# Attention before a gated MLP: products and probability buffers with and without 64 to 192 padding columns

## The chip, the cores and the metric

The kernel runs on one core of a Trainium2 chip. The metric is device time in microseconds (us) for one execution. The engines of a core are named as in the profile: PE is TensorE's matrix multiplication and PEld its loading of the stationary operand (the weights of one product), DVE is VectorE, ACT is ScalarE, POOL is GpSimd, and SP issues the transfers. A product, below, is one matmul instruction: up to 128 x 128 weights, and a moving operand of so many columns.

## The reference

What is computed is block-causal attention over 8 batches of 8 heads, and then a gated MLP on its output:

```python
scores = scale * np.matmul(q, k.transpose(0, 1, 3, 2))      # (8, 8, 576, 576), head_dim 64
mask = block_i >= block_j                                   # blocks of 64 positions
scores = np.where(mask, scores, -1000000000.0)
scores = scores - np.max(scores, axis=-1, keepdims=True)
attn = np.exp(scores)
attn = attn / (np.sum(attn, axis=-1, keepdims=True) + 1e-09)
out = np.matmul(attn, v)                                    # (8, 8, 576, 64)
...
x = out.transpose(0, 2, 1, 3).reshape(4608, 512)
a = x @ w1                                                  # (4608, 1024)
b = x @ w2
h = a * b @ w3
return h @ w_out                                            # (4608, 512)
```

## The kernel before

The heads are taken in 32 pairs, four pairs to a batch. Every float32 value that goes through a product is split in two rounded parts (type fp32r in the profile), a high one and a low one, and products are done as high by high, high by low and low by high. For a head, the tiles `hi` and `lo` hold q and k in this form.

**Scores.** `s_tile` (L226) computes scores transposed, keys on partitions and queries on columns, in five tiles (`S_TILES`, L258): chunk 0 of 128 keys takes two tiles of 288 queries, chunk 1 takes queries 128 to 575, chunk 2 takes 256 to 575, and the fifth tile takes chunk 3 and chunk 4 (64 keys) together. Each part is two products on line L235, one of `hi` and one of `lo`. ACT then takes the exponential twice: to `p` or `rsum` in float32 (L250), and to `ph`, rounded (L251). DVE subtracts the two into `pl`, the low part (L253), and POOL adds `p` to the sums over the keys, `rsum` (L256). Only columns that some query may see are written: chunk 3's exponentials take 192 columns, chunk 4's take 64.

**Probabilities.** `ph` and `pl` have `PW` columns; chunk c begins at `PC[c]`. Between the chunks lie columns of zeros, which POOL writes once (L121), when the tiles of the second stage are opened.

**Values.** `pv` (L281, product on L291) multiplies the values `vs` with `ph` and `pl`, by the list `PV`: chunk 0 in two parts, then chunks 1 to 4. In this version a part of chunk 0, chunk 3 and chunk 4 reach into the zeros, so that each of these products is 256 columns wide. The result gathers in PSUM, in `xps`.

**Order.** The first four pairs (one batch) run while the weights of the MLP come in and are decoded (DVE, L139 to L144); their work is set in order by a scheduler that estimates what each instruction costs, and their values are multiplied in plain float32 (`pv_early`, L275). From pair 4 on, which is the second stage (from some 165 us), PE's order is written out by hand: `PLAN` has one string for the first and one for the second head of a pair; S is a scores tile, V a part of `pv`, F a piece of the MLP (lines L388 and L404), M the maxima of the next pair (`mx`, L182, in bf16), T the sums over the keys (`tot`, L309), and so on. The engines run their instructions in program order, so a product that waits holds all that stands behind it on PE. The MLP lags the attention by a batch, and its last batch stands alone at the end (from some 983 us).

Sums end the pair: DVE transposes `rsum` (`tr`, L304), reduces it (`part`, L305), and PE adds the groups (`tot`, two products of 36 columns). Pair by pair PE's MLP pieces alternate between the first products (`ab`, L388) and the last ones (`o`, L404).

Of the kernel before, what the change touches and what calls it, by code (L numbers as in the profile page):

```python
# [7 lines left out]
F32 = mybir.dt.float32  # L8
# [6 lines left out]
PSUM = bass.MemoryType.PSUM  # L15

P = 128
B, H, S, D = 8, 8, 576, 64
BLK = 64
NB = S // BLK  # L20
NPAIR = H // 2
# [4 lines left out]
NF = DF // P  # L26
HALF = S // 2
RAW = 2 * S + 640
EARLY = NPAIR  # pairs whose work is spread over more engines while the weights come in
SCALE = 0.125  # L30
BIG = 8.0e9

# Columns of a head's probabilities (keys on partitions): a chunk of 128 keys
# takes the queries that may see it; zeros keep every product 256 columns wide.
PC = [128, 704, 1152, 1536, 1920]
PW = 1984
QLO = [0, 128, 256, 384, 512]
# The same without zeros, less the first query.
PE = [0, 448, 768, 960, 1024]


# Order of a head's steps, for the first and the second head of a pair.
PLAN = (
    "B F B F S F S B F F S S F F F S M M V F V V V F R F F V Q N",
    "M A S S A F F S F M M S F F F S M A M V V V F V F F V N Q F R T M F F",
)
# The same for the pairs before the first product of the MLP, while the weights come in.
EARLY_PLAN = (
    "M S S S C S C C C C M S V V B C M M V A V M V M Q B M A B M N",
    "S C C S A S S C S C V V V V V Q N T",  # L50
)
# Steps of the first pair with the MLP beside it that leave the MLP's place empty.
DELAY = 3
# Whether ScalarE makes the roundings of (q and k, q, k, k for the maxima, q for the maxima, v).
CAST = (0, 0, 1, 1, 1, 1)


# [1 line left out]
def block_causal_attention__then__gated_mlp_kernel(ctx, tc, qkv, consts, ident_in, w1, w2, w3t, wout, out_t):  # L59
    nc = tc.nc  # L60
# [4 lines left out]
    work = ctx.enter_context(tc.tile_pool(name="work", bufs=1))  # L65
# [9 lines left out]
    w1l = cpool.tile([P, NC, DF], F32R, name="w1l")  # L75
    wh = cpool.tile([P, NF, DM], F32R, name="wh")
    wl = cpool.tile([P, NF, DM], F32R, name="wl")
    # Per head of a pair: (q, k) with high parts on the head's own half of the
    # partitions and q high, k low on the other; and (q low, k high) on the own
    # half with the rows that shift and mask the scores on the other.  # L80
    hi = [cpool.tile([P, 2, S], F32R, name=f"hi{j}") for j in range(2)]
    lo = [cpool.tile([P, 2, S], F32R, name=f"lo{j}") for j in range(2)]
    w2h = cpool.tile([P, NC, DF], F32R, name="w2h")
    w2l = cpool.tile([P, NC, DF], F32R, name="w2l")
    # Queries of both heads of a pair, block by block on a diagonal.
    qd = cpool.tile([P, NB, P], BF16, name="qd")
    own = [slice(0, D), slice(D, P)]
    oth = [slice(D, P), slice(0, D)]
# [12 lines left out]
    for j in range(2):  # L101
        nc.vector.tensor_copy(lo[j][oth[j]], cst[0:D, 0 : 2 * S].rearrange("p (t s) -> p t s", t=2))
    nc.gpsimd.memset(qd, 0.0)
    # Tiles of the time while the weights come in, and those that take their bytes.
    tl = {}

    def open_early(pool):
# [3 lines left out]
    def open_late():  # L111
        pool = ctx.enter_context(tc.tile_pool(name="late", bufs=1, reuse_waits="tile"))
        tl["late"] = pool
        tl["ph"] = pool.tile([P, PW], F32R, name="ph")
        tl["sum"] = pool.tile([P, S], F32, name="rsum")
        tl["pl"] = pool.tile([P, PW], F32R, name="pl")
        # Values: high part on the columns of the head's own half, low part on the other.
        tl["vs"] = [pool.tile([P, 5, P], F32R, name=f"vs{j}") for j in range(2)]
        for t in (tl["ph"], tl["pl"]):
            for a, b in ((0, PC[0]), (PC[2] + 320, PC[3]), (PC[3] + 192, PC[4])):  # L120
                nc.gpsimd.memset(t[:, a:b].bitcast(F32), 0.0)  # L121
        tl["gh"] = pool.tile([P, NF, HALF], F32R, name="gh")
        tl["gl"] = pool.tile([P, NF, HALF], F32R, name="gl")

    def load_w(dst, src, k):
        """512 columns of float64 words (low, high), as float32.

        Magnitudes below float32's smallest normal become zero.
        """
        t = tl["early"].tile([P, 1024], F32, tag="wraw", name="wraw", bufs=5)  # L130
        u = tl["early"].tile([P, 512], F32, tag="wbits", name="wbits", bufs=6)
        wide = t.bitcast(I32)
        nc.sync.dma_start(out=wide.rearrange("p (k w) -> p k w", k=k), in_=src)
        wide = wide.rearrange("p (c two) -> p c two", two=2)
        low, high = wide[:, :, 0], wide[:, :, 1]
        bits = u.bitcast(I32)
        V = nc.vector
        nc.scalar.activation(u, high.bitcast(F32), AF.Abs)
        V.tensor_scalar(out=u, in0=u, scalar1=2.0**-15, scalar2=None, op0=ALU.max)  # L139
        V.tensor_scalar(out=bits, in0=bits, scalar1=3, scalar2=0x3FFFFFF8, op0=ALU.logical_shift_left, op1=ALU.bitwise_and)  # L140
        V.scalar_tensor_tensor(out=bits, in0=high, scalar=-0x40000000, in1=bits, op0=ALU.bitwise_and, op1=ALU.bitwise_or)  # L141
        if dst is None:
            dst = u.unsqueeze(1)
        V.scalar_tensor_tensor(out=dst.bitcast(I32), in0=low.rearrange("p (k w) -> p k w", k=k), scalar=29,  # L144
                               in1=bits.rearrange("p (k w) -> p k w", k=k), op0=ALU.logical_shift_right, op1=ALU.bitwise_or)
        return u
# [80 lines left out]
    def s_tile(n, j, parts, p_early):  # L227
# [10 lines left out]
        for c, ks, at, q0, q1 in todo:  # L238
# [21 lines left out]
        [(0, 288, 576, 288)],  # L260
        [(1, 128, 576, 128)],
        [(2, 256, 576, 256)],
        [(3, 320, 576, 384), (4, 512, 576, 512)],
    ]
    # (chunk, first column of the probabilities, width, first column in PSUM)
    PV = [(0, 0, 256, 256), (0, PC[0] + 128, 448, 512), (1, PC[1], 448, 512), (2, PC[2], 320, 640),
          (3, PC[3] - 64, 256, 704), (4, PC[4] - 192, 256, 704)]

    def pv_early(n, j, xps, pr):
        for c in range(5):  # L270
# [28 lines left out]
    x_of = {}  # L299

    def sums(n, j, part):
        """Sums over the keys: 32 by 32 transposes, then over the groups of 32 partitions."""
        tr = work.tile([P, S], F32, tag="tr", name=f"tr{n}_{j}")
        nc.vector.transpose(tr, tl["sum"])  # L304
        nc.vector.reduce_sum(part[:, j, :], tr.rearrange("p (b c) -> p b c", c=32), axis=AX.X)  # L305
# [120 lines left out]
    weights = gen_w(wp)  # L426

    def pair(n):
        """The attention of a pair of heads, with what the plan places between its steps."""
        early = n < EARLY  # L430
        x32 = work.tile([P, S], F32, tag="x32", name=f"x32_{n}")
        rr = work.tile([P, S // 32], F32, tag="rr", name=f"rr{n}")
        part = None if early else work.tile([P, 2, S // 32], F32, tag="part", name=f"part{n}")
        last = n + 1 == NN
        masks = iter(()) if last else shift_mask(n + 1)
        own_qk = prep_qk(n, 1)
        next_qk = iter(()) if last else prep_qk(n + 1, 0)
        for j in range(2):
            xps = ps_x.tile([P, 1024], F32, tag="psx", name=f"x{n}_{j}")
            p_early = wp.tile([P, 1600], F32, tag="pe", name=f"pe{n}_{j}") if early else None  # L440
            tiles = iter(S_TILES)
            pvs = (pv_early if early else pv)(n, j, xps, p_early)
            delay = DELAY if n == NPAIR and j == 0 else 0
            for step in (EARLY_PLAN if early else PLAN)[j].split():
                if step == "C":
                    fill(weights, 1)
                    continue
                with tc.high_priority(offset=0) if early else nullcontext():
                    if step == "S":
                        s_tile(n, j, next(tiles), p_early)  # L450
                    elif step == "F":
                        if delay:
                            delay -= 1
                        else:
                            fill(mlp, 1)
                    elif step == "M":
                        fill(masks, 1)
                    elif step == "A":
                        fill(next_qk, 1)
                    elif step == "B":  # L460
                        fill(own_qk, 1)
                    elif step == "V":
                        fill(pvs, 1)
                    elif step == "R":
                        sums(n, j, part)
                    elif step == "N" and early:
                        take_early(n, j, xps, x32, rr)
                    elif step == "N":
                        take(n, j, xps, x32)
                    elif step == "T":  # L470
                        if not early:
                            total(n, part, rr)
                        norm(n, x32, rr)
                        finish_x(n, x32)
                    elif step == "Q" and not last:
                        if n + 1 != NPAIR:
                            prep_v(n + 1, j)
                        if j == 1 and n + 2 < NN:
                            load(n + 2)
# [5 lines left out]
    open_late()  # L485
    for j in range(2):
        prep_v(NPAIR, j)
    # Products of the gated MLP stand between those of the attention, which wait for other engines.
    ctx.enter_context(tc.manual_schedule(engines={mybir.EngineType.PE}))
    mlp = (None for b in range(B - 1) for _ in gen_moe(b))  # L490
    for n in range(NPAIR, NN):
# [52 lines left out]
```

## Time and profile before

| what | value |
|---|---|
| time, median of 3 runs | 1069.15 us (1067.49 to 1069.55) |
| span of the profiled execution, first to last instruction | 1066.6 us |
| the median above that span | 2.55 us |
| PE busy | 986.9 us, 93% |
| DVE busy | 810.3 us, 76% |
| ACT busy | 594.9 us, 56% |
| POOL busy | 601.4 us, 56% |

The profiled execution is shown by its span alone; its time as a run isn't listed, and the 2.55 us are what lies around the span in the median run. Busy times of PE count overlapping matmuls once, and the ends of matmuls are modelled, so starts of successive products tell more than durations do. A wait in brackets behind a row is the engine's idle time ahead of it and what ended it. Times in rows are from the start of the span.

### The profile page before, as it was taken

How to read it: one execution, taken by the hardware profiler on the slowest of the kernel's cores; microseconds unless marked ns; L12 is line 12 of the kernel's file. 1: busy time of each engine (PE TensorE's matmuls, PEld its weight loads, DVE VectorE, ACT ScalarE, POOL GpSimd, SP SyncE). 2: the span in 40 equal slices, each digit the busy share in tenths (PEclk: the TensorE clock that was granted, in tenths of full speed). 3: DMA queues.
4: the chain of work that ended last, by engine and by line, in shares of the span. 5: the costliest groups of instructions: out<-in, count | busy, mean ns of one | idle time of the engine just before them, and what ended most of it. 6: DMA issues, size and time to landing. Idle time of an engine off the chain costs nothing.

```text
span 1066.6 us, 18267 instructions
## 1 busy us (share of the span) xinstructions
PE 986.9 (93%) x6624; PEld 892.7 (84%) x6624; DVE 810.3 (76%) x1432; ACT 594.9 (56%) x1505; POOL 601.4 (56%) x631
## 2 busy tenths in 40 slices
PE   3789778999999999999999999999999999999998
PEld 1444347999998989999999989899999999899998
DVE  7999997878787887778787888877787878886100
ACT  4646566656665656556565656565565656554221
POOL 3324367656575666666565756666665657564211
PEclk9889889999999999999999999999999999999999
DMA  6665421111111001111111110111111111000000
GB/s 214 202 194 191 140 73 36 35 58 36 58 35 54 18 34 47 41 52 36 58 36 58 36 47 19 39 47 42 52 36 58 35 59 36 22 3 18 7 24 23
DMA packets 27196, 61.52 MB, mean 58 GB/s; under 512 B 3361, under 2 KB 19873, under 8 KB 27105
## 3 DMA queue, kind: packets, MB, share of 16 engines
q1 hardware_dynamic: 27104, 60.35, 17.0%
q8 instruction: 52, 0.85, 0.3%
q14 instruction: 40, 0.32, 0.1%
HBM read 50.76 MB, written 9.44 MB: 56 GB/s over the span
## 4 chain that ended last, share of the span: by engine, by line
PE 47%; DVE 34%; ACT 11%; issue 6%; DMA 1%; POOL 1%; ACTq 0%; DVEq 0%; SPq 0%; POOLq 0%
PE ab L388 21%; PE o L404 12%; DVE pl L253 6%; PE s L235 6%; DVE m L186 4%; DVE hi L160 3%; DVE part L305 3%; DVE tr L304 3%; ACT ph L251 3%; DVE g L395 2%; PE x L291 2%; ACT p L250 2%; PE mx L182 2%; PE w L365 2%; DVE wbits L141 2%
## 5 line engine op out<-in xcount | busy, mean ns | idle before, releaser
L256 POOL TENSOR_TENSOR rsum<-rsum,p 128x448 f32<-128x448 f32 x224 | 176.7, 789 | 124.1 <-ACT p L250 116.6
L253 DVE TENSOR_TENSOR pl<-p,ph 128x448 fp32r<-128x448 f32 x168 | 149.1, 901 | 62.2 <-ACT ph L251 61.3
L397 POOL TENSOR_TENSOR gl<-g,gh 128x288 fp32r<-128x288 f32 x128 | 107.5, 840 | 138.0 <-ACT gh L396 135.6
L396 ACT CAST gh<-g 128x288 fp32r<-128x288 f32 x128 | 55.5, 433 | 228.2 <-DVE g L395 228.2
L235 PE MATMUL s<-hi 128*128 128x288 f32 (+4 forms) x384 | 127.8, 344 | 29.0 <-ACT ph L251 21.4
L388 PE MATMUL ab<-xh,w2h 128*128 128x288 f32 x512 | 153.3, 300 | 0.1
L404 PE MATMUL o<-gh,wh 128*128 128x288 f32 x512 | 152.1, 297 | 0.0
L388 PE MATMUL ab<-xh,w1h 128*128 128x288 f32 x512 | 150.9, 295 | 1.1 <-ACT xh L339 1.1
L388 PE MATMUL ab<-xl,w1h 128*128 128x288 f32 x512 | 151.0, 295 | 0.5 <-POOL xl L340 0.5
L388 PE MATMUL ab<-xh,w2l 128*128 128x288 f32 x512 | 150.9, 295 | 0.0
L388 PE MATMUL ab<-xh,w1l 128*128 128x288 f32 x512 | 150.9, 295 | 0.0
L388 PE MATMUL ab<-xl,w2h 128*128 128x288 f32 x512 | 150.9, 295 | 0.0
L404 PE MATMUL o<-gh,wl 128*128 128x288 f32 x512 | 150.8, 295 | 0.0
L404 PE MATMUL o<-gl,wh 128*128 128x288 f32 x512 | 150.7, 294 | 0.0
L186 DVE TENSOR_REDUCE m<-mx 128x1 f32<-128x512 f32 (+6 forms) x320 | 128.1, 446 | 5.0 <-PE mx L182 3.2
L251 ACT ACTIVATE ph<-s 128x288 fp32r<-128x288 f32 x336 | 131.3, 393 | 0.0
L209 POOL TENSOR_TENSOR hi<-raw,hi 64x576 fp32r<-64x576 f32 x64 | 93.7, 1464 | 43.2 <-ACT hi L160 17.8
L291 PE MATMUL x<-ph,vs 128*128 128x256 f32 x336 | 111.6, 340 | 0.1
L250 ACT ACTIVATE p<-s 128x448 f32<-128x448 f32 x224 | 85.4, 381 | 44.6 <-PE s L235 44.3
L235 PE MATMUL s<-lo 128*128 128x288 f32 (+4 forms) x384 | 107.0, 307 | 2.2 <-DMA lo<-ms 1.2
L235 PEld LDWEIGHTS s<-hi 128*128 128x128 f32 (+1 forms) x384 | 70.9, 185 | 45.5 <-ACT ph L251 28.0
L395 DVE TENSOR_TENSOR g<-ab,a 128x288 f32<-128x288 f32 x128 | 57.4, 448 | 66.4 <-PE ab L388 65.5
(77 smaller groups left out, 2558.7 us busy)
## 6 DMA issues: line engine op xcount, KB each, us to landing
raw<-in_qkv SPq DMA_DIRECT2D x32, 896.0 KB
out_t<-o SPq DMA_DIRECT2D x64, 144.0 KB
wraw<-in_w3t SPq DMA_DIRECT2D x16, 512.0 KB
wraw<-in_w SPq DMA_DIRECT2D x16, 512.0 KB
wraw<-in_wout SPq DMA_DIRECT2D x8, 512.0 KB
lo<-ms SPq DMA_DIRECT2D x64, 2.2 KB
cst<-in_consts SPq DMA_DIRECT2D x1, 288.0 KB
ident<-in_ident SPq DMA_DIRECT2D x1, 128.0 KB
```

Source lines behind the costliest of these rows:

```text
L186: nc.vector.reduce_max(m[:, col : col + 1], sc, axis=AX.X)
L209: nc.gpsimd.tensor_tensor(out=hi[j][x, 1, :], in0=rqk[o, 1, :], in1=hi[j][o, 1, :], op=ALU.subtract)
L235: nc.tensor.matmul(t[ks, at : at + q1 - q0], src[:, 1, kr], src[:, 0, q0:q1], start=(s == 0), stop=(s == 1))
L250: nc.scalar.activation(p32, t[ks, at : at + w], AF.Exp, scale=SCALE)
L251: nc.scalar.activation(ph[ks, o : o + w], t[ks, at : at + w], AF.Exp, scale=SCALE)
L253: nc.vector.tensor_tensor(out=low, in0=p32, in1=ph[ks, o : o + w], op=ALU.subtract)
L256: nc.gpsimd.tensor_tensor(out=r, in0=r, in1=p32, op=ALU.add)
L291: nc.tensor.matmul(xps[:, to : to + w], v[:, c, :], pr[:, a : a + w], start=(u < 2 and s == 0), stop=(u in (0, len(PV) - 1) and s == len(p ...
L388: nc.tensor.matmul(t[:, 0:HALF], l[:, c, fs], r, start=(c == 0 and s == 0), stop=(c == NC - 1 and s == 2))
L395: nc.vector.tensor_tensor(out=g32, in0=acc[1][:, 0:HALF], in1=a32, op=ALU.mult)
L397: nc.gpsimd.tensor_tensor(out=gl[:, f, :], in0=g32, in1=gh[:, f, :], op=ALU.subtract)
L404: nc.tensor.matmul(t[:, 0:HALF], l[:, f, es], r[:, f, :], start=(f == 0 and s == 0), stop=(f == NF - 1 and s == 2))
```

## The change

The columns of zeros go. `PC` becomes the running sum of the chunks' own widths and `PW` falls from 1984 to 1600. The six memsets are taken out. In `S_TILES` the fifth tile's part of chunk 3 begins at query 384 in place of 320, so its two products are 192 columns wide in place of 256; what ACT reads of it stays the same. In `PV` the first part of chunk 0 is 128 columns wide in place of 256, chunk 3 is 192 in place of 256, and chunk 4 is 64 in place of 256.

```diff
-PC = [128, 704, 1152, 1536, 1920]
-PW = 1984
+PC = [0, 576, 1024, 1344, 1536]
+PW = 1600
...
         tl["vs"] = [pool.tile([P, 5, P], F32R, name=f"vs{j}") for j in range(2)]
-        for t in (tl["ph"], tl["pl"]):
-            for a, b in ((0, PC[0]), (PC[2] + 320, PC[3]), (PC[3] + 192, PC[4])):
-                nc.gpsimd.memset(t[:, a:b].bitcast(F32), 0.0)
...
-        [(3, 320, 576, 384), (4, 512, 576, 512)],
+        [(3, 384, 576, 384), (4, 512, 576, 512)],
...
-    PV = [(0, 0, 256, 256), (0, PC[0] + 128, 448, 512), (1, PC[1], 448, 512), (2, PC[2], 320, 640),
-          (3, PC[3] - 64, 256, 704), (4, PC[4] - 192, 256, 704)]
+    PV = [(0, 0, 128, 384), (0, 128, 448, 512)] + [(c, PC[c], S - QLO[c], 384 + QLO[c]) for c in range(1, 5)]
```

(The rest of the diff takes comments out, and shifts line numbers by 3 or 4.) From pair 4 on, no engine's order changes: the same instructions stand in the same places, and only widths differ. Before that, the scheduler's estimates of the fifth tile's products change, and with them the order of the first stage. Two places at the seam of the two stages show it. POOL, at the seam, before; `lo_87` is the last head's low part of pair 3, `vs` are the values of pair 4, `xl` the low part of pair 3's output:

```order
L212 TENSOR_TENSOR lo_87<-raw_880,hi_85 64x576
L121 MEMSET ph 128x128
L121 MEMSET ph 128x64
L121 MEMSET ph 128x192
L121 MEMSET pl 128x128
L121 MEMSET pl 128x64
L121 MEMSET pl 128x192
L225 TENSOR_TENSOR vs_1150<-raw_880,vs_1150 128x5x64
L225 TENSOR_TENSOR vs_1151<-raw_880,vs_1151 128x5x64
L340 TENSOR_TENSOR xl_0_1136<-x_3_898,xh_0_1135 128x288
```

POOL at the same place, after (L222 is L225 and L336 is L340 of before): the values follow on `lo_87` at once.

```order
L222 TENSOR_TENSOR vs_1150<-raw_880,vs_1150 128x5x64
L222 TENSOR_TENSOR vs_1151<-raw_880,vs_1151 128x5x64
L336 TENSOR_TENSOR xl_0_1136<-x_3_898,xh_0_1135 128x288
L336 TENSOR_TENSOR xl_1_1140<-x_3_898,xh_1_1139 128x288
L253 TENSOR_TENSOR rsum<-rsum,p_0_1198 128x448
```

ACT, ahead of the seam, before; `w2h` is a rounded piece of a weight, `hi_85` and `lo_87` are those of pair 3's second head, `pe` its exponentials, `kb` and `qd` the bf16 operands for the maxima of pair 5, `xh` the rounded output of pair 3:

```order
L243 ACTIVATE pe_1_1053<-s_1_1088 128x320
L150 CAST w2h<-wbits 128x512
L160 CAST hi_85<-raw_880 64x1152
L243 ACTIVATE pe_1_1053<-s_1_1102 128x192
L243 ACTIVATE pe_1_1053<-s_1_1102 64x64
L160 CAST hi_85<-raw_880 64x576
L192 ACTIVATE ms_1045<-mt_1043 9x128
L160 CAST lo_87<-raw_880 64x576
L160 CAST vs_1150<-raw_880 128x5x64
L160 CAST vs_1151<-raw_880 128x5x64
L160 CAST kb_1258<-raw_1125 128x576
```

ACT at the same place, after (L240 is L243, L157 is L160): `kb` and one `qd` stand ahead of the last exponentials and of `hi_85`, and the `w2h` piece has moved to an earlier place.

```order
L240 ACTIVATE pe_1_1053<-s_1_1088 128x320
L157 CAST kb_1252<-raw_1125 128x576
L157 CAST qd<-raw_1125 64x9x64
L240 ACTIVATE pe_1_1053<-s_1_1102 128x192
L240 ACTIVATE pe_1_1053<-s_1_1102 64x64
L157 CAST hi_85<-raw_880 64x1152
L189 ACTIVATE ms_1045<-mt_1043 9x128
L157 CAST hi_85<-raw_880 64x576
L157 CAST lo_87<-raw_880 64x576
L157 CAST vs_1150<-raw_880 128x5x64
L157 CAST vs_1151<-raw_880 128x5x64
```

## Rows read from the trace of the kernel before

**Rows 1.** The page, part 1: busy time, share of the span, instructions.

```profile
PE 986.9 (93%) x6624; PEld 892.7 (84%) x6624; DVE 810.3 (76%) x1432; ACT 594.9 (56%) x1505; POOL 601.4 (56%) x631
```

**Rows 2.** Busy time by stretch: us, engines' busy us (xcount), granted clock, DMA.

```profile
0.00:165.00 165.00, 123.75 (x376) 66.65 (x376) 149.10 (x251) 96.21 (x182) 67.79 (x51) 0.89 0.50 164
...
500.00:600.00 100.00, 95.38 (x691) 90.79 (x691) 79.89 (x144) 58.65 (x156) 62.93 (x68) 1.00 0.12 41
```

**Rows 3.** The chain that ended last: start us, us, what; two pairs.

```profile
581.23 0.40 ACT a L393
...
593.11 0.66 PE s L235 x2
...
598.45 1.43 PE x L291 x8
...
627.02 0.34 PE s L235 x4
...
633.27 0.41 PE tot L309 x2
```

**Rows 4.** Who waited for whom: us in total, times, longest us.

```profile
PE s L235 <- ACT ph L251: 21.4, 27, 0.8
...
PE tot L309 <- DVE part L305: 7.7, 13, 0.6
```

**Rows 5.** PE's groups by shape: weights, moving operand, xcount | busy us, mean ns.

```profile
L291 PE MATMUL x<-ph,vs 128*128 128x256 f32 x168 | 55.8, 332 | 0.1
...
L291 PE MATMUL x<-pl,vs 128*128 128x256 f32 x112 | 34.3, 307 | 3.7 <-DVE pl L253 3.6
...
L235 PE MATMUL s<-lo 128*64 128x64 f32 x64 | 14.3, 224 | 0.0
...
L235 PE MATMUL s<-hi 128*64 128x64 f32 x64 | 12.4, 194 | 0.0
```

**Rows 6.** PE in order of time, fifth scores tiles of second heads, and `tot`.

```profile
597.59 0.28 PE L235 MATMUL s<-hi 128*128 128x256 f32 x1
...
597.83 0.19 PE L235 MATMUL s<-hi 128*64 128x64 f32 x1
...
603.26 0.30 PE L309 MATMUL tot<-part,ident 128*128 128x36 f32 x2
603.40 0.28 PE L190 MATMUL mt<-ident,m 128*9 128x128 f32 x1
...
626.86 0.28 PE L235 MATMUL s<-hi 128*128 128x256 f32 x1
...
627.09 0.19 PE L235 MATMUL s<-hi 128*64 128x64 f32 x1
```

**Rows 7.** Instructions on tile `tot`: durations min/median/max in ns.

```profile
L309 PE MATMUL tot<-part,ident x56: 193/275/300, 192.0 to 982.7; 128*128 128x36 f32 x56
```

**Rows 8.** PE, values of an early head in plain float32, in order of time.

```profile
67.09 1.67 PE L275 MATMUL x<-pe,ve 128*128 128x448 f32 x4
```

**Rows 9.** The chain that ended last, at the seam of the two stages.

```profile
165.56 0.49 POOL ph L121 x3
166.05 0.43 POOL pl L121 x3
...
166.56 2.21 POOL vs L225 x2
168.77 0.76 POOL xl L340
```

**Rows 10.** ACT at the seam, in order of time.

```profile
161.34 1.15 ACT L160 CAST hi<-raw 64x1152 fp32r<-64x1152 f32 x1 [0.84 <-PE s L235]
...
165.10 0.67 ACT L160 CAST kb<-raw 128x576 bf16<-128x576 f32 x1
...
168.08 0.77 ACT L339 CAST xh<-x 128x288 fp32r<-128x288 f32 x2 [0.28 <-DVE x L330]
```

## The prediction

> **What bounds the kernel now.** I read the page first, then busy times by stretch, then the chain of work that ended last, then PE's waits, and only then single products. PE is busy 93% of the span [rows 1], and in the second stage some 95 us of every 100 at the full granted clock, 2.4 GHz [rows 2]. Before 165 us DVE is the busiest, 149 of 165 us, so that PE's width matters little there. A share of 95% looks like a PE limit, but the chain says otherwise for part of each pair. Take the pair at 581 us. From 581.23 to 593.11 the chain runs through ACT and DVE alone [rows 3]: a copy, exponentials, subtractions, the casts and sums of the first head. It ends where PE, having run its own products of that head, sits idle until ACT frees a scores buffer. That wait comes 27 times in 28 pairs and takes 0.8 us [rows 4]. So in every pair PE already has 0.8 us to spare at the end of the first head, and what PE saves there makes this wait longer, not the kernel shorter. From 593.11 on the chain is PE's. There are two kinds of second heads. In ten pairs the eight products of the values (598.45) stand in the chain, so PE sets the end all through the second head. In the other 18 the chain leaves PE after the fifth scores tile (627.02), goes over ACT and DVE, and comes back at `tot` (633.27); there PE waits up to 0.6 us for DVE, 13 times [rows 3, 4], and savings in the values only lengthen that wait.
>
> **The narrower products.** Per head of the second stage (56 heads) seven products shrink: the two of scores chunk 3 from 256 to 192, `ph` and `pl` of chunk 0's first part from 256 to 128, `ph` and `pl` of chunk 3 from 256 to 192, and `ph` of chunk 4 from 256 to 64. (The five of the values are three of the 168 and two of the 112 per 56 heads in [rows 5].) What does one cost? Two 256-wide ones follow each other in 0.24 us (597.59 to 597.83) or 0.23 (626.86 to 627.09), so 0.117 us each, or 0.46 ns a column [rows 6]. It is tempting to multiply: 704 columns fewer per head are 0.32 us.
>
> But each product also has weights of its own to load, and the trace shows what that costs when a product is too short to hide it. The `tot` products are 36 columns wide with 128 columns of float32 weights. Together they take 0.14 us (603.26 to 603.40) [rows 6], and the duration is 193 ns for one whose weights are there and 275 ns for the usual second one [rows 7]: it stood 82 ns for its weights, after the first one's 0.03 us of streaming. So 128 columns of weights take about 0.113 us, counted from the start of the product before. The fifth tile says the same at half the size: its 64-wide products have 64 columns of weights, the first takes 194 ns and the second 224 [rows 5], 30 ns late after 0.03 us of streaming, so 64 columns of weights take about 0.059 us. A product then costs the longer of its own columns and the next product's weights. A 256-wide one, 0.117, lies just above the 0.113 of a full load of weights; anything narrower falls to 0.113 and no further.
>
> The Trainium skill, "TensorE: Matmul & The Clock Gate", section "LDWEIGHTS (loading the stationary operand)", gives a load as its columns divided by 1.2 GHz, 107 ns for 128; the trace's 113 ns is near it. By the page's figure a narrow product would save 10 ns in place of 4 or 5, and the sum below would be some 0.5 us larger.
>
> So, per head: the first product of scores chunk 3 is followed by a full load: 117 less 113, about 5 ns (between 0 and 10). The second is followed by a load of 64 columns, 0.059 us, which 192 columns (0.088 us) cover: it saves 30 ns. The five of the values are each followed by a full load, 5 ns each. Scores 35 ns, values 25 ns. On the path: ten second heads with both, 0.60 us; 18 with the scores alone, 0.63 us; first heads nothing. Their largest gain is chunk 4's in a first head, which a bf16 product follows, and it ends in the 0.8 us wait. Sum 1.23 us, with ends at 0.5 (full loads cost as much as 256 columns) and 5.7 (every head counted, the first ones' chunk 4 with 88 ns).
>
> **The memsets and the seam.** The six memsets take 0.49 and 0.43 us on POOL, and the chain passes through them: memsets, then `vs`, then `xl`, for which PE's first MLP products wait [rows 9]. They are gone, but not all of 0.95 us is gained. `xl` needs `xh`, which ACT starts at 168.08, when DVE has finished `x` [rows 10]; its first half is there at about 168.4, and `xl` now starts at 168.77. So at most 0.35 us. Against it stands the new order on ACT: `kb` and one `qd`, 0.67 us each, now run ahead of the last exponentials and of the cast to `hi`. In the trace ACT sat idle 0.84 us ahead of that cast, waiting for PE [rows 10], and the 0.6 us of `w2h` have left this place, so between nothing and 0.5 us of the 1.34 is uncovered; POOL's `hi`, `lo` and `vs` come that much later and lose up to half of what the memsets gave, and `xl` still finds `xh` as the later one. I take 0.35 us gained, between 1.0 gained and 1.3 lost. The other shifts of order in the first stage add no work to any engine; I take nothing for them. The smaller buffers move the addresses of tiles opened after them, and all that held those bytes is done by then.
>
> **Sum.** 1.23 + 0.35 is 1.6 us. The profiled span goes from 1066.6 to 1065.0, and the median of the runs, 2.55 us above the span before, to 1067.6, which is 0.15% less. A measurement of this kernel can tell about 0.2%, or 2.1 us, from no change; this is below.
>
> **The rivals.** *Columns set the price.* If the next weights were hidden whatever the width, a head would save its 704 columns, 0.32 us: ten second heads give 3.2 us, the other 18 give their scores' 0.06 each, 1.1 us, and with the seam the time is 1064.5; were the first heads' wait to shrink as well, 56 heads give 18 us and 1051. For it speaks that 64-wide products show 0.03 us of streaming; against it the 82 ns that `tot` waits [rows 7]. The Trainium skill, same page, section "Back-to-back issue gap", has such a formula for single products, columns over 2.4 GHz plus 2.5 ns: 704 columns would be 0.29 us a head, which would give about this rival's time; `tot`'s 36 columns, at 0.113 us, are not priced so.
>
> *Narrow products fall back to the plain float32 pace* (the other side). Early heads multiply the same values in plain float32, and there four instructions for 448 columns take 1.67 us less the last one's 0.16 of draining [rows 8]: two instructions a product, 0.377 each, or 1.68 ns a column. If rounded products narrower than 256 went at that pace, 192 columns would cost 0.32 us (0.2 more than now, four times a head), 128 columns 0.215 (0.1 more, twice) and 64 columns with two loads 0.22 (0.1 more): 1.1 us a head, 32 us for the second heads and up to 63 for all, 1101 to 1132. It decides from the first narrow product on. Against it: the 64-wide scores products are rounded, too, and show 0.03 and 0.06 us.
>
> *The first stage drifts.* The new order in it (ACT's casts above, DVE's maxima between the decoding steps) costs 1 to 4 us ahead of the seam: 1069 to 1072. No row shows a wait that would grow so; but DVE is 90% busy there [rows 2], so a step that is late is not caught up.
>
> **How the numbers follow.** Weights set the pace, as summed: 0.70, from 1064.9 to 1069.3. Columns: 0.13. Drift: 0.12. Float32's pace: 0.05. The range reaches from 1064.4, which takes in the nearer half of the columns' case, to 1070.0, which takes in over half of the drift: 0.82 inside. Faster by over 0.2%: a quarter of the first case and all of the second, 0.31. Slower: a third of the drift, and float32's pace, 0.09. The rest, 0.60, is the same.
>
> **What would show it.** In the trace after, `ph` to `pl` of chunk 0's first part should start 0.11 us apart, not 0.06; the two scores products of chunk 3 should together take 0.20 us in place of 0.24; PE's wait for ACT's `ph` should rise from 0.8 to about 0.9 us in each pair; PE busy should fall by 2 to 5 us with most of it turned into idle time; `xl` should follow `xh` and not `vs`. A start-to-start of 0.06 us, or a span shorter by over 3 us, would prove the weights' price wrong; a wait at the end of the first head that doesn't grow would prove the slack wrong; a seam later than 169.6 us would prove the second term wrong.

## The result, and the profile after

The changed kernel takes 1072.12 us (median of 16 runs, 1068.25 to 1073.88), the kernel before on the same chip 1068.57 us (16 runs, 1067.28 to 1069.55). The ratio is 1.0029, 95% interval 1.0019 to 1.0039: slower by 3.1 us by that ratio (the medians lie 3.55 us apart), where 1067.6 us was forecast with a range of 1064.4 to 1070.0. The prediction was wrong, and on the wrong side of the kernel before. One thing is needed to read the times: those of the changed kernel spread over 5.6 us and go with the mean granted clock of the run (1068.25 to 1069.45 us at 0.986 or 0.987, 1069.66 to 1072.02 at 0.984, 1071.26 to 1073.88 us at 0.981 or 0.982); the profile shown here is one at 0.981.

The page after, busy time by engine, and two stretches (us from the start; stretch length; busy PE, PEld, DVE, ACT, POOL with their instructions; granted clock; DMA share; GB/s), to be held against [rows 1, 2]:

```profile
PE 979.9 (92%) x6624; PEld 887.9 (83%) x6624; DVE 808.4 (76%) x1432; ACT 594.9 (56%) x1505; POOL 594.8 (56%) x625
...
0.00:165.00 165.00, 117.55 (x359) 63.07 (x360) 147.52 (x246) 92.38 (x175) 61.53 (x49) 0.88 0.49 164
500.00:600.00 100.00, 94.46 (x685) 89.75 (x685) 79.66 (x141) 57.90 (x155) 62.81 (x68) 1.00 0.12 41
```

PE does 7.0 us less. But by 165 us every engine has done less than before: DVE, the busiest of that stretch, 147.5 us instead of 149.1, and POOL 61.5 instead of 67.8. The first stage is late.

Two marks split the span: `tot` of pair 4, the first pair of the second stage, and `tot` of pair 31, the last one. They stand here for before and then for after (start, length, engine, line, operation):

```profile
191.96 0.30 PE L309 MATMUL tot<-part,ident 128*128 128x36 f32 x2
...
982.69 0.31 PE L309 MATMUL tot<-part,ident 128*128 128x36 f32 x2
```

```profile
196.77 0.30 PE L305 MATMUL tot<-part,ident 128*128 128x36 f32 x2
...
986.52 0.30 PE L305 MATMUL tot<-part,ident 128*128 128x36 f32 x2
```

So the second stage between the marks went from 790.73 to 789.75 us, 0.98 less. All that lies behind the second mark is 83.9 us in both. What lies ahead of the first mark grew by 4.81 us. The sum is 3.8 us, the difference of the spans (1066.6 and 1070.4). **A gain near the forecast one is there, and a loss five times its size stands ahead of it.** For the rest one more mark is used: the last early transpose `tr<-x` on DVE, that of pair 3's second head, with which the first stage ends.

At the seam the chain of waits of after reads (start, length, what was on the chain), to be held against [rows 9, 10]:

```profile
159.75 1.36 PE x L271 x4
...
162.49 1.65 PE s L232 x4
...
167.37 1.99 PE x L271 x8
...
169.38 0.79 DVE tr L312
...
173.04 0.44 ACT xh L335
...
173.55 0.81 POOL xl L336
...
174.40 0.40 PE ab L384
```

As forecast, the memsets and `vs` are off this chain and `xl` follows `xh`. But `ab` starts at 174.40 us, 4.8 us later than before, and the chain comes over PE's steps to a `tr` that waits for them. DVE's waits up to 170 us, of before and then of after (engine, line, tile, what it waited for: us in total, times, longest):

```profile
DVE m L186 <- PE mx L182: 3.2, 4, 1.4
DVE tr L316 <- PE x L275: 3.0, 3, 2.4
DVE wl L354 <- ACT wh L353: 1.9, 1, 1.9
```

```profile
DVE tr L312 <- PE x L271: 6.6, 4, 3.3
...
DVE m L183 <- PE mx L179: 3.4, 3, 1.7
DVE wl L350 <- ACT wh L349: 3.3, 3, 2.4
```

DVE has the same instructions in both, in another order, and in these rows it waits 5.2 us more: 3.6 for the early value products, 1.4 for `wh`, which ACT copies out of PE's products of the weights, and 0.2 for the maxima.

### The profile page after: what moved, and what is told of

Its sections match the earlier page's. It is cut to its first block, busy times and chain, and to the rows that moved or that the text cites. A ratio compares the mean times of both kernels' runs of the same rounds, so it can differ in the third digit from the quotient of the medians.

```text
span 1070.4 us, 18255 instructions
## 1 busy us (share of the span) xinstructions
PE 979.9 (92%) x6624; PEld 887.9 (83%) x6624; DVE 808.4 (76%) x1432; ACT 594.9 (56%) x1505; POOL 594.8 (56%) x625
## 4 chain that ended last, share of the span: by engine, by line
DVE 42%; PE 36%; ACT 13%; issue 8%; DMA 1%; ACTq 0%; POOL 0%; DVEq 0%; SPq 0%
PE ab L384 13%; PE o L400 12%; DVE pl L250 8%; PE s L232 5%; DVE m L183 5%; DVE hi L157 4%; DVE g L391 4%; DVE part L301 4%; DVE tr L300 3%; ACT ph L248 3%; ACT p L247 3%; DVE wbits L138 2%; DVE ph L250 2%; PE w L361 2%; ACT xlow L319 2%
## 5 line engine op out<-in xcount | busy, mean ns | idle before, releaser
L250 DVE TENSOR_TENSOR pl<-p,ph 128x448 fp32r<-128x448 f32 x168 | 147.5, 891 | 62.1 <-ACT ph L248 61.3
L232 PE MATMUL s<-hi 128*128 128x288 f32 (+4 forms) x384 | 125.2, 337 | 31.2 <-ACT ph L248 24.1
L391 DVE TENSOR_TENSOR g<-ab,a 128x288 f32<-128x288 f32 x128 | 57.4, 448 | 67.8 <-PE ab L384 63.4
L287 PE MATMUL x<-ph,vs 128*128 128x128 f32 x336 | 104.2, 319 | 0.3 <-ACT ph L248 0.2
```

Of the source, the lines that this page charges most:

```text
L232: nc.tensor.matmul(t[ks, at : at + q1 - q0], src[:, 1, kr], src[:, 0, q0:q1], start=(s == 0), stop=(s == 1))
L250: nc.vector.tensor_tensor(out=low, in0=p32, in1=ph[ks, o : o + w], op=ALU.subtract)
L287: nc.tensor.matmul(xps[:, to : to + w], v[:, c, :], pr[:, a : a + w], start=(u < 2 and s == 0), stop=(u in (0, len(PV) - 1) and s == len(p ...
L391: nc.vector.tensor_tensor(out=g32, in0=acc[1][:, 0:HALF], in1=a32, op=ALU.mult)
```

## The experiments

Times in the expectations that come from single starts count from the first busy instruction, 0.2 us behind the zero of the rows here.

### Which stage, and order or width

The scheduler orders the first stage by what it estimates for each instruction. The early heads use `S_TILES` too, so narrowing the fifth tile changed both the width of 16 products there and the order of everything. Four kernels take these apart; in each the order on every engine is that of before or that of after.

**The late change alone:** the early heads keep their 256-wide products, and so the order of before.

```diff
+    S_EARLY = S_TILES[:4] + [[(3, 320, 576, 384), (4, 512, 576, 512)]]
...
-            tiles = iter(S_TILES)
+            tiles = iter(S_EARLY if early else S_TILES)
```

> The change in the second stage alone: in the first four pairs the fifth score tile keeps its 256-wide products, and the order of instructions on every engine is that of the kernel before; from pair 4 on products, buffers and memsets are as after. Theory (the loss is made in the first stage, by the other order of its steps): the MLP's first product starts at 168.5 to 170.0 us as before, the stretch from pair 4's product of the sums to pair 31's is 789.8 us (790.7 before, 789.8 after), and the median is 0.7 to 1.5 us under the kernel before, near 1067.5. Rival (narrow products make the second stage or the memory's layout dearer in a way that one profile did not show): 2 to 4 us over the kernel before, near 1072, as after.

Measured: 1067.67 us (11 runs) against 1068.57, ratio 0.9992 (0.9983 to 1.0, so just at the edge of no change). The MLP's product that waits for pair 3 starts at 168.08 us, a little sooner than the range given, and between the marks lie 790.04 us. The loss is gone; the gain is what the second stage gives.

**The early change alone:** the kernel before, where only the early heads take the narrow tile.

```diff
+    S_EARLY = S_TILES[:4] + [[(3, 384, 576, 384), (4, 512, 576, 512)]]
...
-            tiles = iter(S_TILES)
+            tiles = iter(S_EARLY if early else S_TILES)
```

> The change in the first stage alone: in the first four pairs the fifth score tile's products of chunk 3 are 192 wide and the order on every engine is that of the changed kernel; from pair 4 on all is as in the kernel before (256 wide, memsets, 1984 columns). Theory (first stage's order): the MLP's first product starts 3.5 to 5.5 us later than before, 173 to 175 us, the second stage takes 790.7 us as before, and the median is 3 to 5 us over the kernel before, 1071.5 to 1073.5. Rival (the loss is in the second stage): no slower than before, within 0.5 us.

Measured: 1074.14 us (6 runs), ratio 1.0053 (1.0041 to 1.0065). That product starts at 175.23 us, and between the marks lie 790.79 us, as before. The loss is in the first stage, even a little above the range given.

**Narrow early products in the order of before.** The program is ordered with 256-wide products; then the finished instructions are made narrower.

```diff
+            if [list(x) for x in out.ap][-1] != [1, 256]:
+                continue
...
+                ap[-1] = [1, 192]
+                new.append(copy.replace(p, ap=ap, offset=p.offset + (64), bass_ap=None))
```

> As the kernel with the late change alone, in the same order on every engine, but the 16 products (8 heads, two each) of the first stage's fifth score tile are narrowed to 192 columns after the order had been set: width of after, order of before. Theory (order, not width): within 0.7 us of the kernel with the late change alone, about 1067.5, MLP's first product at 168.5 to 170.0 us. Rival (the width itself slows the first stage, through the granted clock or the products' own price): 3 to 5 us over it, near 1072.

Measured: 1066.50 us (11 runs), ratio 0.9982 (0.9974 to 0.9991). Its profile has the product at 169.72 us. The median is a little further from the late change alone than expected (1.2 us, not 0.7), and on the fast side.

**Wide early products in the order of after:** the changed kernel, with the opposite edit behind the ordering.

```diff
+            if [list(x) for x in out.ap][-1] != [1, 192]:
+                continue
...
+                ap[-1] = [1, 256]
+                new.append(copy.replace(p, ap=ap, offset=p.offset + (-64), bass_ap=None))
```

> The changed kernel with its order on every engine, but the same 16 products of the first stage widened to 256 columns after the order had been set: width of before, order of after. Theory (order, not width): as the changed kernel, 1071 to 1073 us, MLP's first product at 173 to 175 us. Rival (width): 1067 to 1068.5 us, MLP's first product at 168.5 to 170.0 us.

Measured: 1071.60 us (12 runs), ratio 1.0033 (1.0021 to 1.0045), product at 173.19 us. Put together, with each profile's last `tr<-x`, DVE's busy time ahead of it and the difference of the two:

| kernel | order of | early width | last `tr<-x` | DVE busy | DVE idle | between the marks | median |
|---|---|---|---|---|---|---|---|
| before | before | 256 | 164.32 | 148.42 | 15.9 | 790.73 | 1068.57 |
| late change alone | before | 256 | 163.14 | 148.85 | 14.3 | 790.04 | 1067.67 |
| narrow, order of before | before | 192 | 164.72 | 148.53 | 16.2 | 790.01 | 1066.50 |
| early change alone | after | 192 | 169.87 | 148.34 | 21.5 | 790.79 | 1074.14 |
| after | after | 192 | 169.38 | 148.52 | 20.9 | 789.75 | 1072.12 |
| wide, order of after | after | 256 | 167.95 | 149.59 | 18.4 | 789.82 | 1071.60 |

The stretch up to `tr<-x` in three of these profiles (stretch, its length, DVE's busy time with its instructions, granted clock, DMA share, GB/s): before, narrow in the order of before, after.

```profile
0.00:164.32 164.32, 148.42 (x250) 0.89 0.50 164
```

```profile
0.00:164.72 164.72, 148.53 (x251) 0.89 0.49 164
```

```profile
0.00:169.38 169.38, 148.52 (x250) 0.88 0.48 160
```

The order decides, and no loss follows the width: the three kernels in the order of before end the first stage at 163.1 to 164.7 us, the three in that of after at 168.0 to 169.9. DVE's busy time hardly differs, so at this mark, which is itself a step of DVE, the loss is idle time on DVE.

### Is the order's price a draw?

If the price comes from the accident of the order, other orders should fall anywhere. Two kernels have the 16 products counted as 224 and as 240 columns when the order is set, and run them 192 wide.

```diff
-    S_EARLY = S_TILES[:4] + [[(3, 320, 576, 384), (4, 512, 576, 512)]]
+    S_EARLY = S_TILES[:4] + [[(3, 352, 576, 384), (4, 512, 576, 512)]]
```

> As the kernel with narrow products in the order of before, but the order of the first stage is the one the scheduler gives when those 16 products are counted as 224 columns wide; they run 192 wide. A third order, which no run had so far. Theory (the order is a draw, paid in VectorE's idle time): pair 4's product of the sums starts at 174.7 to 176.9 us plus VectorE's waits up to 175 us (six kernels so far: 15.5 to 21.2 us of waits, start at 190.2 to 197.4), second stage 789.8 to 790.1 us, and the time may fall on either side of before, 1066 to 1074. Rival (a fewer counted column costs steadily more): half way between the orders of 256 and 192, tot of pair 4 at 193.5 to 194.5, median 1068.5 to 1070.

> The same with the 16 products counted as 240 columns wide when the order is set, and run 192 wide: a fourth order. Theory (a draw): as for 224, the start of pair 4's product of the sums follows VectorE's waits and need not lie between its neighbours. Rival (steady in the counted width): a quarter of the way from the order of 256 to that of 192, tot of pair 4 at 192 to 193.5, median 1067.5 to 1069.

Measured, against 1068.76 us for before: counted as 224, 1069.50 us (10 runs, ratio 1.0009, 0.9999 to 1.0018), `tr<-x` at 164.80 with 15.2 us of idle time; counted as 240, 1075.28 us (4 runs, ratio 1.0057, 1.0037 to 1.0077), `tr<-x` at 171.90. With the same 192-wide products, the early order was counted as 256, 240, 224 and 192 columns; `tr<-x` came at 164.7, 171.9, 164.8 and 169.4 us, `tot` of pair 4 at 192.1, 199.7, 193.6 and 196.8 us, and the medians are 1066.50, 1075.28, 1069.50 and 1072.12 us. That is no trend, and the worst order is a neighbour of the best. It takes 240 to put the steady rival out, which had 1067.5 to 1069 there; for 224 its forecast was met (1068.5 to 1070, and `tot` within 0.2 us of its 193.5 to 194.5). The mark `tr<-x` hides what 224 costs: behind it a small step of DVE (`rr<-tr`) took 1.31 us beside POOL's `lo` in place of 0.43, and PE's granted clock was 0.74 from 171 to 176 us, where it was 1.00 in the order of before. My rule that the start follows DVE's waits held for 224 only just (`tot` of pair 4 at 193.6) and failed for 240 (199.7 us): there DVE was idle for 19.9 us, less than in after, but busy for 152.0 us over the same 250 instructions. Why they took 3.5 us longer is not settled; 1.1 us of it are one step, `x<-x,rb`, which stood beside POOL's `w2l` for 1.82 us and ran clear of POOL in 0.75 us in after.

### Is DVE's time paid one for one?

In the changed kernel's order every fifth of DVE's 40 lower bounds on the weights' magnitudes was cut to 64 columns.

```diff
+            if getattr(i, "op0", None) != ALU.max or not (i.outs[0].memref or "").startswith("wbits"):
+                continue
+            seen += 1
+            if seen % 5:
+                continue
...
+                ap[-1] = [1, 64]
```

> The changed kernel, where every fifth of VectorE's 40 lower bounds on the weights' magnitudes (0.56 us each over 512 columns) takes 64 columns, set after the order was: eight of them, 3 to 4 us of VectorE's work in the first stage; the clamp to a smallest magnitude is left out for the other columns. Theory (VectorE bounds the first stage, each us on it is paid): pair 3's second transpose starts at 165 to 166.7 us (168.9 to 169.3 in three profiles of the changed kernel), the end 2.5 to 3.8 us earlier at the same clock. Rival (transfers or TensorE set the pace and VectorE only waits for them): 168 us or later, and VectorE's idle time up by 2.5 us or more.

The stretch ahead of this kernel's last `tr<-x` (its end is that start), DVE busy alone:

```profile
0.00:164.78 164.78, 146.26 (x251) 0.91 0.49 164
```

DVE is busy for 146.3 us and idle for 18.5, and the mark comes at 164.78. Two more profiles of the changed kernel, at a mean clock of 0.982 and 0.984 (this one: 0.984), have 148.9 and 149.3 us of work, 18.9 and 19.0 of idle time and the mark at 167.77 and 168.29. So the mark comes 3.0 to 3.5 us sooner, and 3.0 us sooner than in any of six profiles of the changed kernel (167.77 to 170.52); that is a little ahead of the theory's range. The run took 1067.63 us, the two others 1070.86 and 1070.50. The idle time did not grow, so the rival is out: transfers and PE didn't hold DVE back by more when it had less to do, and what was taken from DVE was taken from the first stage. The size is not clean. A step of 512 columns takes 0.42 us where nothing disturbs it and one of 64 columns 0.18, so that the cut takes 1.9 us of work proper, and the mark moved by more; the last section has a reason why DVE's times vary.

### What DVE waits for

If DVE waits for PE's late results, taking PE's work away should close the gap between the orders. The 64 products `w<-wo,w`, PE's largest load in the first stage, kept 64 of their 512 columns (but for the first of each eight), in both orders.

```diff
+            if name != last:
+                last = name
+                continue
...
+                assert ap[-1] == [1, 512], ap
+                ap[-1] = [1, 64]
```

> The kernel with narrow products in the order of before, with TensorE's largest load of the first stage taken out: of the 64 products of 512 columns that make the output's weights (62 us of TensorE in the first stage) all but the first of each eight keep only 64 columns, set after the order was; the output is not the reference's. To be read against its twin in the order of after. Theory (the order costs because VectorE, which bounds the first stage, waits in its queue for TensorE's and ScalarE's results): with TensorE early, VectorE's waits for TensorE shrink, pair 3's second transpose on VectorE (164.5 us in this order without the cut) starts at 156 to 161 us. Rival (the order costs by something else): at 162 to 165 us.

> The changed kernel with the same cut of the products that make the output's weights; the output is not the reference's. Theory (VectorE waits for late results of TensorE): pair 3's second transpose, 4.7 us later than in the order of before without the cut (169.15 against 164.48 us), is now less than 1.7 us later than in the twin. Rival (the order costs by ScalarE, GpSimd or the transfers): still 3.5 to 5 us later.

DVE's waits in the order of before and then in that of after, both with light products:

```profile
DVE tr L313 <- PE x L272: 4.3, 3, 3.4
...
DVE m L183 <- PE mx L179: 2.0, 3, 1.4
```

```profile
DVE tr L312 <- PE x L271: 7.5, 4, 4.1
...
DVE m L183 <- PE mx L179: 2.3, 2, 1.7
```

The waits for `wh` (1.8 and 3.3 us) are gone from both. The order of before gained only 0.5 us (last `tr<-x` 164.72 to 164.19), where the theory wanted 4 to 8; that lies in the rival's range, so in this order the late PE is not the limit. The order of after gained 3.1 us (169.38 to 166.29). The gap fell from 4.7 to 2.1 us, between the theory's 1.7 and the rival's 3.5; by `tot` of pair 4 it fell from 4.7 to 3.1 us (191.20 and 194.28). So a third to a half of the loss goes with PE's weight products. What is left goes with the wait of `tr` for the value products, 3.2 us longer in this order; that is read from the waits and was not tested. What makes these products late was not separated, and the granted clock confuses this pair: it fell to 0.77 and 0.75 over the stretch (0.89 and 0.88 without the cut), so that the steps left on PE ran slower.

### The clock

The changed kernel was profiled five times more, for a run at a mean clock of 0.986.

> The changed kernel as it is, for a second profile. Its 16 totals went with the granted clock's mean: 1068.3 to 1069.7 us where that was 0.984 to 0.987, 1071.1 to 1073.9 us at 0.981 to 0.984; those of before hardly did. Theory (in the new order TensorE's lateness stands on the way to the second stage, so what the clock takes in the first stage is paid in full): a profile with a mean clock of 0.986 or more has VectorE's waits for TensorE shorter by 2 us or more than the 10.0 us (transposes and maxima) of the first profile, and pair 4's product of the sums at 192.5 to 194.5 us; one at 0.981 repeats 196 to 198 us. Rival (the clock is not the cause): 195.5 us or later at either clock.

> The changed kernel once more, for a third profile; expected as for the second one, by the clock that it is granted.

> The changed kernel once more. If the profile falls at a mean clock of 0.986 or more, theory: VectorE's idle time ahead of pair 3's second transpose is 18.5 us or less and pair 4's product of the sums starts at 192.5 to 194.5 us; at 0.981 as the three before it, 196.4 to 196.6 us. Rival (the clock is not the cause): 195.5 us or later at either.

> The changed kernel once more, by the clock it is granted, as for the fourth look.

> The changed kernel once more, by the clock it is granted, as for the fourth look.

None fell there. With the clock at 0.979, 0.981 (twice), 0.982 and 0.984, `tot` of pair 4 started at 198.3, 196.6, 196.9, 195.5 and 195.8 us, and DVE was idle for 21.0, 20.6, 21.0, 18.9 and 19.0 us. Later times go with lower clocks, as in the theory, but all of them lie in the rival's range, 195.5 us or later, or at most 0.2 us ahead of it, and the case that would decide, 192.5 to 194.5 us at 0.986, was never seen. Nor do these runs tell cause from effect: a first stage in which PE waits for longer may itself lower the mean clock. What the rows show is where the clock would bite. Ten microseconds of after at the seam, and the stretch of before at the lower clock:

```profile
156.50:166.50 10.00, 7.56 (x26) 5.37 (x26) 6.31 (x15) 7.12 (x16) 4.28 (x4) 0.50 0.01 3
```

```profile
157.50:160.90 3.40, 3.10 (x13) 2.56 (x13) 2.16 (x8) 2.72 (x6) 0.69 (x2) 0.54 0.01 2
```

In after, PE runs at 1.2 GHz for 10 us, and for most of them its steps are on the chain; in before for some 3.4 us there; over the first 165 us the mean granted clock hardly differs (0.88 and 0.89). That the faster third of the changed kernel's runs owes its 3 to 4 us to this stays open.

### Which narrowed products count

The prediction gave second heads the gain and first heads nothing. Two kernels have narrow products in one kind of head only, from pair 4 on, with order, zeros and buffers of before.

```diff
-            tiles = iter(S_TILES)
+            tiles = iter(S_NARROW if not early and j == 1 else S_TILES)
...
-        for u, (c, a, w, to) in enumerate(PV):
+        for u, (c, a, w, to) in enumerate(PV_NARROW if j == 1 else PV):
```

> The kernel before with narrow products only in the second heads of the pairs from 4 on (zero columns and buffers are kept, order and first stage are those of before). From pair 4's product of the sums to pair 31's, before took 790.73 and 790.79 us and four kernels with all products narrow 789.76 to 790.04. Theory (only work between the last wait of a pair and its product of the sums counts): this kernel alone brings the whole gain, 789.8 to 790.1 us, 0.06 us in each pair that takes 28.7 us and nothing in the pairs of 30.0 us. Rival (every narrowed product counts the same): half of it, 790.3 us.

> The kernel before with narrow products only in the first heads of the pairs from 4 on; order and first stage are those of before. Theory (first heads have slack at the wait for ScalarE's high probabilities, which grows from 0.8 to 0.9 us): 790.6 to 790.85 us from pair 4's product of the sums to pair 31's, as before, and the wait for ScalarE longer by 0.06 us a pair. Rival (every narrowed product counts the same): 790.3 us.

The marks and PE's waits (200 to 980 us) with narrow second heads:

```profile
191.73 0.30 PE L311 MATMUL tot<-part,ident 128*128 128x36 f32 x2
...
981.56 0.30 PE L311 MATMUL tot<-part,ident 128*128 128x36 f32 x2
```

```profile
PE s L235 <- ACT ph L251: 20.5, 26, 0.8
PE tot L311 <- DVE part L307: 8.2, 13, 0.6
PE x L293 <- DVE pl L253: 3.6, 14, 0.3
```

And with narrow first heads:

```profile
191.00 0.30 PE L311 MATMUL tot<-part,ident 128*128 128x36 f32 x2
...
981.64 0.31 PE L311 MATMUL tot<-part,ident 128*128 128x36 f32 x2
```

```profile
PE s L235 <- ACT ph L251: 23.1, 26, 0.9
PE tot L311 <- DVE part L307: 7.7, 13, 0.6
PE x L293 <- DVE pl L253: 4.0, 14, 0.3
```

789.83 us against 790.64, with 790.73 before: the second heads bring the whole gain, the first heads 0.1 us. In the same stretch of before:

```profile
PE s L235 <- ACT ph L251: 20.6, 26, 0.8
PE tot L309 <- DVE part L305: 7.7, 13, 0.6
PE x L291 <- DVE pl L253: 3.6, 14, 0.3
```

What the first heads save turns up as 2.5 us more waiting for `ph` and 0.4 more for `pl`. The slack was read rightly. The sums between the marks scatter by some tenths from profile to profile (five more of the changed kernel gave 788.96 to 789.71 us), but the kind of pair that gains is plain in the medians: 28.71 us before, 28.66 with narrow second heads, 28.72 with narrow first heads.

## Why the prediction was wrong

**The step that failed** is the sentence "The other shifts of order in the first stage add no work to any engine; I take nothing for them." Its first half is true of DVE: its work ahead of the mark is 148.4 and 148.5 us. The second half doesn't follow. DVE bounds this stage and takes its queue in order, so a wait on it delays all that stands behind. The new order cost 4.8 us, and by DVE's waits it did so by putting `tr` and `wl` where their inputs weren't there yet; that the order is the cause was tested, the way from the order to these waits only in part. The prediction also says that no row shows a wait that would grow so. The trace of before does: DVE is idle for 15.9 us ahead of the mark, 8.1 of them in the three waits shown above, and these three grew. The rival had the mechanism and the reason ("a step that is late is not caught up"), with 1 to 4 us and a chance of 0.12. That chance was too small: the order behaved like a draw here, and of the three new orders tried two lost 4.7 and 7.6 us by `tot` of pair 4 and one 1.5. None gained. I priced the steps that I saw move at the seam and took the rest for nothing. The order of before was the best of the four; how often another kernel's first order is so good, four orders can't tell.

**The narrow products** came out as worked out. The weights set the pace (after, PE, start and length; [rows 6] has the same place before):

```profile
631.06 0.25 PE L232 MATMUL s<-hi 128*128 128x192 f32 x1
631.15 0.28 PE L232 MATMUL s<-lo 128*128 128x192 f32 x1
631.26 0.19 PE L232 MATMUL s<-hi 128*64 128x64 f32 x1
...
631.72 0.30 PE L287 MATMUL x<-ph,vs 128*128 128x128 f32 x1
631.86 0.27 PE L287 MATMUL x<-pl,vs 128*128 128x128 f32 x1
631.97 0.42 PE L287 MATMUL x<-ph,vs 128*128 128x448 f32 x1
```

Chunk 3's two scores products take 0.20 us together, as forecast; from the first 128-wide value product to the second lie 0.14 us by their starts and 0.11 by their ends, and 0.11 to the one behind. None shows the 0.06 us of 128 streamed columns, so the rival by columns falls. The Trainium skill, "TensorE: Matmul & The Clock Gate", section "Back-to-back issue gap", gives its formula by columns for an isolated product, and says that in a stream of loads and products both set the spacing; the trace agrees with the second, but the page's figure there for 128 columns, about 81 ns, is below the 0.11 us here. Plain float32's pace falls too.

**The split over second heads** was off, and the errors partly cancelled. I gave ten of them 0.06 us and 18 of them 0.035, by the chain; the waits of [rows 4] had already counted only 13 pairs in which PE waits at `tot`. The interval from `tot` to `tot` shows two kinds of pairs: those of 28.71 us (median) went to 28.67, by about 0.06 us in nearly every one of them, the whole of what scores and values save; those of 30.01 us stayed at 30.01. In these PE's savings went into its waits, 0.4 us more for `pl` and 0.5 more for `part` in all. The 0.035 us of the scores, which I counted as gained there, was not. So 14 pairs at 0.06 us, 0.84, against 1.23 forecast; the sums of the table give 0.7 to 1.0, with the scatter told above. PE's busy time fell by 7.0 us, where 2 to 5 was forecast; the difference, in records that overlap, was not followed up. Two sums in the prediction were off beside this: with full loads as dear as 256 columns, 28 second heads would still save 30 ns each, 0.84 us and not 0.5; and the range of its first case, 1064.9 to 1069.3, is narrower than the ends of its terms add up to (1062.5 to 1070.0).

**The memsets' place** was sized well: from the last `tr<-x` to `tot` of pair 4, 27.6 us in the three kernels with zeros in the order of before, 27.3 and 27.4 in the two without, 0.3 us against 0.35 forecast. This rests on the order of before, where each of the two groups agrees within 0.07 us; in the order of after the same distance runs from 27.4 to 27.8 us over six profiles of one kernel. My test for it was badly chosen, though: "a seam later than 169.6 us" is met (174.40), but what it shows is the first stage. A mark at the end of a stage can't judge a term that is a part of it; the distance from the last step ahead of the term can.

**The sum** of 1.6 us was good wherever the order stayed: 0.9 us (0.0 to 1.8) with the late change alone, 1.9 us (1.0 to 2.8) with the early products narrowed as well. That last version, 1066.50 us, beats both kernels: the same change, with the first stage's order held.

## What to carry to other kernels

Where a scheduler sets the order from estimates, an edit to a shape that it sees can redraw the order of the whole stage; look whether the order moved on the engine that bounds the stage, and then give the redraw a range of its own, from the idle time that this engine already shows. Three redraws cost 1.5 to 7.6 us here, of a stage that had 15.9 us of idle time. Hold the order and change the size, or the reverse, before believing either. And a product that already ends before the next weights are loaded (0.11 us for 128 columns of them here) gains nothing by being narrower still.

## What the runs showed of the hardware

The time of some of DVE's steps depends on what POOL does meanwhile. The same decoding steps over 512 columns, in after, first on DVE and then what POOL ran meanwhile (start, length):

```profile
29.14 0.42 DVE L136 TENSOR_SCALAR wbits<-wbits 128x512 f32<-128x512 f32 x1
...
30.05 1.86 DVE L138 SCALAR_TENSOR_TENSOR wbits<-wraw,wbits 128x512 int32<-128x512 int32 x1
31.84 1.62 DVE L136 TENSOR_SCALAR wbits<-wbits 128x512 f32<-128x512 f32 x1
```

```profile
29.96 1.41 POOL L206 TENSOR_TENSOR hi<-raw,hi 64x576 fp32r<-64x576 f32 x1 [16.49 <-ACT hi L157]
31.44 1.73 POOL L209 TENSOR_TENSOR lo<-raw,hi 64x576 fp32r<-64x576 f32 x1
```

The step that takes 0.42 us alone takes 1.62 beside POOL's subtraction and ends shortly behind it (33.46 and 33.17 us). In the first stage of after 55 of these two steps of the decoding (L136 and L137) ran clear of POOL and none took over 0.43 us; 25 ran beside it, with a median of 0.90 and up to 1.63 us, some 13 us more in all than as many clear ones. The Trainium skill, "Trainium Architecture — The Big Picture", section "What this means for kernel authors", says that DVE and GpSimd share a pair of ports under an exclusive lock; these rows agree. It also blurs the cut of eight DVE steps: their mean of 0.56 us was partly POOL's time, and cut to 64 columns they still took 0.49 us on average, 0.18 where POOL was away, up to 1.42 where it was not. DVE's busy time is thus no fixed quantity either, and may be how the order counted as 240 columns came by the rest of its 3.5 us; that was not tested.
